# Four sums of a small tail, done one by one among the next expert's first steps

## The chip, the core and the metric

The kernel runs on one core of a Trainium2 chip. The metric is the device time of one execution in microseconds (us), less being better. The engines are PE (matrix products; PEld is its weight load), DVE (vector), ACT (activation), POOL and SP (which here mostly start DMAs). Each works through its own instructions in order; they wait for one another through semaphores. PSUM is the memory into which PE writes its results.

## What is computed

Attention with a local window and block summaries gives 3072 rows of 512; then comes a mixture of eight experts, each token going to two of them. The change lies in the experts:

```python
def _moe_ref(x, w_gate, w_noise, noise, w1, w2):
    ...
    for e in range(E):
        for k in range(2):
            mask = top2[:, k] == e
            ...
            h = np.maximum(x[mask] @ w1[e], 0.0)
            out[mask] += top2_w[mask, k, None] * (h @ w2[e])
    return out.astype(np.float32)
```

## The kernel before

Attention and the choice of experts come first (the first quarter of the time), then the experts one after the other, `e` from 0 to 7, sorted by how many tokens they have. `CAPS` (line 38) gives each a number of slots: 800, 832, 808, 800, 784, 776, 768, 768. The slots are worked in chunks of 128; what goes beyond six chunks is the **tail**, chunk 6 (`LAST`). Experts 3, 4 and 5 have tails of 32, 16 and 8 slots. Expert 0 has one of 32 as well, experts 1 and 2 have tails of 64 and 40 that go another way, and experts 6 and 7 have none.

All matrices are split into a high and a low half of 16 bits, and three products of halves make one product. The first layer of experts 2 to 7 (`seven`, line 1370) is a scheme of seven products on half-sized blocks, in four steps `i` = 0 to 3. In this document **(i,u)** is product u of step i. PE does them in this order: (0,1) and (0,5) ahead of the tail of the expert before (`seven_head`, line 1581), then, behind that tail, (0,2), (0,6), and for each i from 1 on (i,1), (i,5), (i−1,7), (i,2), (i,6), (i−1,3), (i−1,4). Each is six matmuls into a bank of PSUM. Between products, other engines read and rewrite those banks:

- after (i,2), (i,3) and (i,4), ACT writes the high half `hth` (L1392) and DVE the low half `htl` (L1395);
- after (i,6), DVE adds ACT's copy `p` of (i,5) to what stands in (i,6)'s bank and writes the sum into the bank of (i,3) (`h<-h,p`, L1386); (i,7), which goes on in (i,6)'s bank, may not start before that is done;
- after (i,7), DVE makes the sum `rh` (L1388), which ACT and DVE then halve;
- (i+2,5) starts afresh in the bank of (i,3), so it waits for both halves of (i,3).

The second layer (`mm2_part`, line 1417) makes a chunk's 128 rows in one PSUM tile `pt`. `mm2_out` (line 911) has DVE multiply it by the token's weight and add the earlier output `prev` (gathered by POOL), and POOL scatters the result `y` to the output.

For a tail of at most 32 slots (`four`, line 780) the matmuls for hidden columns f, f+4 go to a quarter of PE of their own. So the result stands as four partial sums in the four groups of 32 partitions of `pt`, and DVE adds them up: instruction `g` reads partitions 32g to 32g+n, multiplies by the weight, and adds `prev` (g = 0) or the `y` so far (L920). After the fourth comes the scatter.

The order is written out by hand. `on(t, f, ...)` puts a piece of work at place t of an expert's plan, and `hook(t)` does what stands there (pieces of one place in the order in which they were asked for). Place 3 lies behind (0,2), 4 to 6 behind (0,6), 7 and 8 behind (1,1) and (1,5), 9 behind (0,7), 10 behind (1,2), 11 behind (1,6), 12 behind (0,3), 13 behind (0,4); 14 to 20 lie likewise in the next step. DVE's other work at these places is the low halves of the expert's second-layer weights (`w2l`, L758, places 4, 7, 14, 21) and sums and low halves of the next expert's tokens (`xt`, L1293 to L1297, places 9, 11, 12; `x`, L1323, places 15, 16, 18, 19). The gathers of `prev` for the expert's first chunks stand at places 17, 20 and 23; a gather waits for the scatters of the expert before.

Of the kernel before, what the change touches and what calls it, by code (L numbers as in the profile page):

```python
# [25 lines left out]
E, F = 8, 1024  # L26
# [37 lines left out]
def attn_moe(ctx, tc, qt, kt, vt, wgn, noise, w1, w2, out):  # L64
# [23 lines left out]
    def indirect(**kw):  # L88
        nc.gpsimd.memset(spacer, 0.0)
        return nc.gpsimd.indirect_dma_start(**kw)  # L90
# [689 lines left out]
    def four(e, c):  # L780
        return c == LAST and CAPS[e] - LAST * P <= 32

    def tb_of(e, c):
        return TB0[:, c] if e == 0 and c < 3 else TB[:, e, c]
# [3 lines left out]
    def chunks(e):  # L788
        return -(-CAPS[e] // P)
# [78 lines left out]
        return lows  # L868

    ow = {}  # L870
    pi_ = [0]

    def prev_gather(e, c):
# [37 lines left out]
    def mm2_out(e, c, py, pv):  # L911
        last = c == LAST
        if four(e, c):
            n = CAPS[e] - LAST * P
            y = late[0].tile([P, DM], F32, name="y", bufs=4)[:n]
            gw = tb_of(e, c).bitcast(F32)[:n, 1:2]
            for g in range(4):
                x = py[32 * g:32 * g + n]
                if g or pv is not None:
                    nc.vector.scalar_tensor_tensor(y, x, gw, y if g else pv[:n], op0=OP.mult, op1=OP.add)  # L920
                else:
                    nc.vector.tensor_scalar(y, x, gw, None, op0=OP.mult)
            y_scatter(e, c, y)
            return
        d = HD if last else DM
        y = late[0].tile([P, DM], F32, name="y", bufs=4)[:, :d]
        gw = (TL[:, e] if last else tb_of(e, c)).bitcast(F32)[:, 1:2]
        if pv is None:
            nc.vector.tensor_scalar(y, py[:, :d], gw, None, op0=OP.mult)
        else:  # L930
            nc.vector.scalar_tensor_tensor(y, py[:, :d], gw, pv[:, :d], op0=OP.mult, op1=OP.add)  # L931
        y_scatter(e, c, y)
# [7 lines left out]
    def y_scatter(e, c, y):  # L940
        last = c == LAST and not four(e, c)
        n = CAPS[e] - LAST * P if four(e, c) else P
        s = indirect(
            out=out2 if last else out,
            out_offset=bass.IndirectOffsetOnAxis(ap=IL[:, e:e + 1] if last else tb_of(e, c)[:n, 0:1], axis=0),
            in_=y, in_offset=None, bounds_check=(2 * N if last else N) - 1, oob_is_err=False)
        for o in ow.get(e, []):
            tc.declare_no_dep(s.ins, o.ins, reason="an expert's slots hold different tokens")
        ow.setdefault(e, []).append(s)
# [449 lines left out]
    def seven_head(e):  # L1399
        if e == 2:  # L1400
            banks_init()
        seven(e, 0, 1)
        seven(e, 0, 5)
# [60 lines left out]
    def on(t, f, *a):  # L1464
        plan.setdefault(t, []).append((f, a))

    def hook(t):
        for f, a in plan.pop(t, []):
            f(*a)

    def plan_w1(n, p, t, *u):
        on(t, w_load, n, p)
        on(u[0], w1_sums, n, p)
        for i in range(2):
            on(u[1 + i], w1_hi, n, p, i)
        for i in range(2):
            on(u[3 + i], w1_lo, n, p, i)

    def plan_x(n, g, t, s, h, l):
        if t is not None:  # L1480
            on(t, xs_gather, n, g)
        for i in range(3):
            on(s[i], xs_sums, n, g, i)
        for i in range(2):
            on(h[i], xs_hi, n, g, i)
        for i in range(4):
            on(l[i], xs_lo, n, g, i // 2, i % 2)

    for e in range(1, E):
        pv = []  # L1490

        def prev():
            if len(pv) < chunks(e):
                pv.append(prev_gather(e, len(pv)))

        n = e + 1
        if e == 1:
            on(0, tail_ids)
            plan_x(n, 0, 0, (3, 3, 3), (4, 4), (5, 5, 5, 5))
            plan_x(n, 1, 1, (6, 6, 6), (7, 7), (8, 8, 8, 8))  # L1500
            plan_w1(n, 0, 1, 9, 9, 10, 10, 10)
            plan_w1(n, 1, 2, 11, 11, 12, 12, 12)
            plan_x(n, 2, 7, (13, 13, 13), (14, 14), (15, 15, 15, 15))
            plan_w1(n, 2, 11, 33, 33, 34, 34, 34)
            plan_x(n, 3, 12, (35, 35, 35), (36, 36), (37, 37, 37, 37))
            plan_w1(n, 3, 13, 38, 38, 39, 39, 39)
        else:
            for i, (a, b) in enumerate(((3, 4), (4, 7), (8, 14), (15, 21))):
                on(a, w_hi, e, 4 + i)
                on(b, w_lo, e, 4 + i)  # L1510
            on(36, tail_next, e)
            if n < E:
                plan_x(n, 0, None, (9, 11, 12), (10, 13), (15, 16, 18, 19))
                plan_x(n, 1, None, (22, 23, 25), (24, 27), (28, 29, 29, 31))
                plan_w1(n, 0, 8, 32, 32, 33, 33, 34)
                plan_w1(n, 1, 15, 35, 35, 36, 36, 37)
                plan_x(n, 2, 20, (38, 38, 38), (39, 39), (40, 40, 40, 40))
                plan_w1(n, 2, 35, 41, 41, 42, 42, 43)
                plan_x(n, 3, 32, (44, 44, 44), (45, 45), (46, 46, 46, 46))
                plan_w1(n, 3, 38, 47, 47, 48, 48, 49)  # L1520
            if e > 2:
                on(4, w_load, e, 6)
                on(4, w_load, e, 7)
        if n + 1 < E:
            on(40 if e == 1 else 43, xs_gather, n + 1, 0)
            on(42 if e == 1 else 47, xs_gather, n + 1, 1)
        if n < E:
            on(44, w_load, n, 4)
            on(44, w_load, n, 5)
        if e == 1:  # L1530
            on(48, w_load, n, 6)
            on(48, w_load, n, 7)
        for t in (17, 20, 23):
            on(t, prev)
        if e == 1:
            for half in range(2):
                for f in range(FC):
                    mm1(e, half, f)
                    hook(8 * half + f)
            for t in range(16, 32):  # L1540
                hook(t)
        else:
            hi, lo = seven(e, 0, 2)
            hi()
            lo()
            hook(3)
            seven(e, 0, 6)
            for t in range(4, 7):
                hook(t)
            for i in range(1, 5):  # L1550
                if i < 4:
                    seven(e, i, 1)
                    hook(7 * i)
                    seven(e, i, 5)
                    hook(7 * i + 1)
                h7 = seven(e, i - 1, 7)
                h7[0]()
                hook(7 * i + 2 if i < 4 else 28)
                if i < 4:
                    h2 = seven(e, i, 2)  # L1560
                    h2[0]()
                    h7[1]()
                    hook(7 * i + 3)
                    seven(e, i, 6)
                    h2[1]()
                    hook(7 * i + 4)
                else:
                    py = psum.tile([P, 512], F32, name="pt", bufs=2)
                    mm2_part(e, 0, py, 0, range(7), True, False)
                    h7[1]()  # L1570
                    hook(29)
                h3 = seven(e, i - 1, 3)
                h3[0]()
                hook(7 * i + 5 if i < 4 else 30)
                h4 = seven(e, i - 1, 4)
                h4[0]()
                h3[1]()
                h4[1]()
                hook(7 * i + 6 if i < 4 else 31)
        for c in range(chunks(e)):  # L1580
            if c == chunks(e) - 1 and n < E:
                seven_head(n)
            if c or e == 1:
                py = psum.tile([P, 512], F32, name="pt", bufs=2)
                for i, k in enumerate((0, 2, 1)):
                    if e == 1:
                        mm2_pass(e, c, py, k, 1)
                    else:
                        mm2_part(e, c, py, k, range(FC), i == 0, i == 2)
                    if i < 2:  # L1590
                        hook(32 + 3 * c + i)
            else:
                for k in (2, 1):
                    mm2_part(e, 0, py, k, range(7), False, False)
                    hook(33 - k // 2)
                for k in (0, 2, 1):
                    mm2_part(e, 0, py, k, (7,), False, k == 1)
            mm2_out(e, c, py, pv[c])
            prev()
            hook(34 + 3 * c)  # L1600
        for t in range(60):
            hook(t)
# [104 lines left out]
```

## Time and profile before

| what | value |
|---|---|
| time, median of 3 runs | 643.7 us (642.26 to 645.98) |
| profiled execution | 650.73 us |
| its span, first to last instruction | 648.9 us |
| mean granted PE clock in the span | 0.989 |

The profile is that of one execution. Its parts: the page with each engine's busy time and the chain that ended last; the timeline, in which a row has the start (us from the span's start), the length, the engine, line and operation, result and operands with their shape, the count, and in brackets the idle time of the engine just before and what ended it; and the busy time in stretches. Neighbouring instructions of one kind are one row of the timeline. PE's ends are modelled, so its waits are better read from starts.

### The profile page before, as it was taken

The numbers are of one execution on the slowest core, as the hardware profiler recorded it, in microseconds if no ns is written. First come the engines' busy times: TensorE is split into PE (matmuls) and PEld (weight loads), VectorE is DVE, ScalarE is ACT, GpSimd is POOL, SyncE is SP. The second block draws the span as 40 slices with busy tenths as digits, with TensorE's granted clock in tenths as the row PEclk, the third lists the DMA queues.
The fourth block names the chain that finished last, engine by engine and source line by source line (L and its number), as shares of the span: only waits on it lengthen the run. The fifth ranks groups of instructions, "written<-read, shape, count | busy, mean of one in ns | idle before, by whom it ended". The sixth has DMA issues, their size and how long they took to land.

```text
span 648.9 us, 14149 instructions
## 1 busy us (share of the span) xinstructions
PE 628.6 (97%) x5295; PEld 363.4 (56%) x5295; DVE 481.2 (74%) x1039; ACT 316.1 (49%) x692; POOL 250.2 (39%) x432
## 2 busy tenths in 40 slices
PE   8989898999999999999999999999999999999995
PEld 7778676765554554465446544554454455445542
DVE  5768598979887599368887887988798679767510
ACT  4878597973054354065436433653465256425300
POOL 4352043202335353623572356326632542333041
PEclk9999798999999999999999999999999999999998
DMA  9999978963639595838786688769776868763021
GB/s 304 325 278 342 307 218 275 299 230 124 198 123 252 166 220 144 282 84 170 185 226 172 168 200 246 181 135 225 236 201 136 221 210 165 175 191 123 3 94 51
DMA packets 123709, 127.93 MB, mean 197 GB/s; under 512 B 83242, under 2 KB 86674, under 8 KB 123630
## 3 DMA queue, kind: packets, MB, share of 16 engines
q1 hardware_dynamic: 111838, 90.66, 52.1%
q0 software_dynamic: 11792, 36.27, 18.2%
q8 instruction: 44, 0.72, 0.5%
q14 instruction: 35, 0.29, 0.2%
HBM read 81.85 MB, written 25.61 MB: 166 GB/s over the span
## 4 chain that ended last, share of the span: by engine, by line
PE 86%; DVE 6%; ACT 3%; DMA 2%; issue 2%; SPq 1%; POOL 0%; POOLq 0%; DVEq 0%; ACTq 0%
PE pt L1432 29%; PE h L1360 16%; PE h L854 10%; PE pt L909 7%; PE pt L1360 3%; PE pt L341 3%; PE o L1360 3%; PE s L318 3%; PE o L354 3%; PE h L909 2%; PE o L246 1%; ACT p L333 1%; PE pt L378 1%; DMA vd<-in_vt_dram 1%; DVE y L920 1%
## 5 line engine op out<-in xcount | busy, mean ns | idle before, releaser
L90 POOL DMA_INDIRECT out_dram<-y,tb x52 | 69.5, 1336 | 165.3 <-DVE y L931 127.7
L90 POOL DMA_INDIRECT xg<-xd,tb x54 | 60.9, 1127 | 118.8 <-DVE rh L1388 31.5
L1432 PEld LDWEIGHTS <-hth 128*128 128x128 f16 x576 | 56.3, 98 | 66.7
L931 DVE SCALAR_TENSOR_TENSOR y<-pt,tb,prev 128x512 f32<-128x512 f32 x42 | 31.5, 749 | 64.9 <-PE pt L1432 54.2
L1360 PEld LDWEIGHTS <-w1h 128*128 128x128 f16 x504 | 48.9, 98 | 38.2 <-issue 4.4
L1432 PE MATMUL pt<-w2l,hth 128*128 128x512 f16 x288 | 69.0, 379 | 0.0
L1432 PE MATMUL pt<-w2h,htl 128*128 128x512 f16 x288 | 69.0, 379 | 0.0
L1432 PE MATMUL pt<-w2h,hth 128*128 128x512 f16 x288 | 69.0, 379 | 0.0
L1360 PEld LDWEIGHTS <-w1l 128*128 128x128 f16 x504 | 49.3, 98 | 34.9
L90 POOL DMA_INDIRECT prev<-out_dram,tb x45 | 52.6, 1169 | 23.9 <-issue 13.2
L333 ACT ACTIVATE p<-s,nm 128x120 f32<-128x120 f32 x192 | 51.1, 377 | 0.8
L854 PE MATMUL h<-xte,w1h 128*128 128x384 f16 (+2 forms) x248 | 49.1, 336 | 0.0
L1432 PEld LDWEIGHTS <-htl 128*128 128x128 f16 x288 | 28.2, 98 | 34.0
L1349 ACT ACTIVATE w1h<-stg 128x768 f16<-128x768 f32 (+1 forms) x24 | 22.7, 944 | 40.6 <-DVE stg L1340 40.6
L1392 ACT ACTIVATE hth<-h 128x384 f16<-128x384 f32 (+4 forms) x48 | 23.8, 497 | 35.5 <-PE h L1360 35.5
L1349 ACT ACTIVATE w1l<-stg 128x768 f16<-128x768 f32 (+1 forms) x24 | 22.5, 942 | 37.3 <-DVE stg L1340 37.3
L1360 PE MATMUL h<-xte,w1h 128*128 128x384 f16 (+4 forms) x180 | 39.7, 329 | 0.7 <-DVE h L1386 0.4
L1360 PE MATMUL h<-xte,w1l 128*128 128x384 f16 (+4 forms) x180 | 39.7, 329 | 0.0
L1313 ACT ACTIVATE x<-xt 128x512 f16<-128x512 f32 (+2 forms) x44 | 26.5, 626 | 23.4 <-issue 19.2
L1340 DVE TENSOR_TENSOR stg<-stg 128x256 f32<-128x256 f32 x96 | 36.3, 419 | 0.8
L344 ACT ACTIVATE pts<-pt 120x512 f32<-120x512 f32 x48 | 26.7, 609 | 19.4 <-PE pt L341 19.4
L854 PEld LDWEIGHTS <-w1h 128*128 128x128 f16 x256 | 24.7, 98 | 19.5 <-issue 1.2
(301 smaller groups left out, 1305.7 us busy)
## 6 DMA issues: line engine op xcount, KB each, us to landing
stg<-in_w_dram SPq DMA_DIRECT2D x64, 512.0 KB
q<-in_qt_dram SPq DMA_DIRECT2D x24, 256.0 KB
xd<-x SPq DMA_DIRECT2D x24, 256.0 KB
out_dram<-xg SPq DMA_DIRECT2D x8, 768.0 KB
kb<-in_kt_dram SPq DMA_DIRECT2D x6, 768.0 KB
hth<-in_vt_dram SPq DMA_DIRECT2D x12, 260.0 KB
htl<-in_vt_dram SPq DMA_DIRECT2D x16, 195.0 KB
ve<-in_vt_dram SPq DMA_DIRECT2D x12, 260.0 KB
```

Of the source, the lines that this page charges most:

```text
L90: return nc.gpsimd.indirect_dma_start(**kw)
L333: nc.scalar.activation(PE_[t][:, a, hp, :], SC[t][:, a, hp, :], AF.Exp, bias=NM[t][:, 1, a, hp:hp + 1], scale=0.125)
L344: nc.scalar.activation(PT[t][:NK, a], pt[:NK], AF.Copy)
L854: nc.tensor.matmul(ph[:, :n], w1_of(w, wn, c, f), x[:, xo + c, c0:c1], start=(k == 0), stop=(k == 11))
L909: nc.tensor.matmul(py, hx[:, f, c * P:c * P + P], wv[:, f, :], start=st, stop=sp)
L931: nc.vector.scalar_tensor_tensor(y, py[:, :d], gw, pv[:, :d], op0=OP.mult, op1=OP.add)
L1313: nc.scalar.activation(t[:r, c:c + k], src, AF.Copy)
L1340: nc.vector.tensor_tensor(o, x, y, op=op)
L1349: nc.scalar.activation(hi, x, AF.Copy, scale=W1S)
L1360: nc.tensor.matmul(ph[:, :h], w[:, la, a, P * j:P * j + P], x[:, j, :h], start=start and k == 0, stop=k == 5, skip_group_check=True)
L1392: nc.scalar.activation(hh[:, f, t], src, AF.Relu)
L1432: nc.tensor.matmul(py, x, wv[:, f, :], start=st, stop=sp, skip_group_check=True)
```

## The change

For tails of at most 32 slots of the experts 1 to 6 (in effect 3, 4 and 5) `mm2_out` no longer asks for the four sums and the scatter. It keeps four closures in `late_sums`, and the plan of the next expert takes them up at places 5, 8, 10 and 13; the scatter comes with the fourth. The tail of expert 0 stays as it was.

```diff
     ow = {}
+    late_sums = []
     pi_ = [0]
...
             n = CAPS[e] - LAST * P
             y = late[0].tile([P, DM], F32, name="y", bufs=4)[:n]
             gw = tb_of(e, c).bitcast(F32)[:n, 1:2]
-            for g in range(4):
+
+            def part(g):
                 x = py[32 * g:32 * g + n]
                 if g or pv is not None:
                     nc.vector.scalar_tensor_tensor(y, x, gw, y if g else pv[:n], op0=OP.mult, op1=OP.add)
                 else:
                     nc.vector.tensor_scalar(y, x, gw, None, op0=OP.mult)
-            y_scatter(e, c, y)
+                if g == 3:
+                    y_scatter(e, c, y)
+
+            for g in range(4):
+                if 0 < e < E - 1:
+                    late_sums.append((part, g))
+                else:
+                    part(g)
             return
...
                 on(a, w_hi, e, 4 + i)
                 on(b, w_lo, e, 4 + i)
+            for t in (5, 8, 10, 13):
+                if late_sums:
+                    f, g = late_sums.pop(0)
+                    on(t, f, g)
             on(36, tail_next, e)
```

The order of instructions shows it on DVE. Line numbers of the changed kernel are 9 higher from here on (L1395 becomes L1404; L920 becomes L922). At the end of expert 4, DVE had this before; `y` is the sum, `pt_6513` the tail's result, `htl<-o` belongs to (0,2) of expert 5, `h<-h,p_6511` to (0,6), `rh` and `htl<-rh` to (0,7), `h<-h,p_6584` to (1,6):

```order
L920 SCALAR_TENSOR_TENSOR y_6538<-pt_6513,tb_182,prev0_2968 16x512
L920 SCALAR_TENSOR_TENSOR y_6538<-pt_6513,tb_182,y_6538 16x512 x3
L1395 SCALAR_TENSOR_TENSOR htl_90<-o_2882,hth_89 128x388
L1386 TENSOR_TENSOR h_4482<-h_4480,p5_6511 128x388
L758 SCALAR_TENSOR_TENSOR w2l0_322<-stg_6408,w2h0_321 128x1024
L758 SCALAR_TENSOR_TENSOR w2l0_322<-stg_6410,w2h0_321 128x1024
L1388 TENSOR_TENSOR rh1_3827<-h_4480,p5_6511 128x388
L1293 TENSOR_TENSOR xt_6607<-xg0_165 128x512
L1395 SCALAR_TENSOR_TENSOR htl_90<-rh1_3827,hth_89 128x388
L1386 TENSOR_TENSOR h_4483<-h_4481,p5_6584 128x388
```

All four sums stood ahead of everything of the new expert. At the same place it now has:

```order
L1404 SCALAR_TENSOR_TENSOR htl_90<-o_2882,hth_89 128x388
L1395 TENSOR_TENSOR h_4482<-h_4480,p5_6511 128x388
L758 SCALAR_TENSOR_TENSOR w2l0_322<-stg_6408,w2h0_321 128x1024
L922 SCALAR_TENSOR_TENSOR y_6538<-pt_6513,tb_182,prev0_2968 16x512
L758 SCALAR_TENSOR_TENSOR w2l0_322<-stg_6410,w2h0_321 128x1024
L922 SCALAR_TENSOR_TENSOR y_6538<-pt_6513,tb_182,y_6538 16x512
L1397 TENSOR_TENSOR rh1_3827<-h_4480,p5_6511 128x388
L1302 TENSOR_TENSOR xt_6601<-xg0_165 128x512
L1404 SCALAR_TENSOR_TENSOR htl_90<-rh1_3827,hth_89 128x388
L922 SCALAR_TENSOR_TENSOR y_6538<-pt_6513,tb_182,y_6538 16x512
L1395 TENSOR_TENSOR h_4483<-h_4481,p5_6577 128x388
```

Sums 0, 1 and 2 have moved behind the add of (0,6), into the stretch that ends with the low half of (0,3). The second place is a little further on, again on DVE; before, behind that low half (the first row, of (0,3); the second is of (0,4)):

```order
L1395 SCALAR_TENSOR_TENSOR htl_90<-h_4482,hth_89 128x388
L1395 SCALAR_TENSOR_TENSOR htl_90<-h_4480,hth_89 128x388
L758 SCALAR_TENSOR_TENSOR w2l0_322<-stg_6565,w2h0_321 128x1024
L1323 TENSOR_TENSOR x_6669<-xg0_165,x_6618 128x512
L1388 TENSOR_TENSOR rh1_3827<-h_4481,p5_6584 128x388
```

and now:

```order
L1404 SCALAR_TENSOR_TENSOR htl_90<-h_4482,hth_89 128x388
L1404 SCALAR_TENSOR_TENSOR htl_90<-h_4480,hth_89 128x388
L922 SCALAR_TENSOR_TENSOR y_6538<-pt_6513,tb_182,y_6538 16x512
L758 SCALAR_TENSOR_TENSOR w2l0_322<-stg_6557,w2h0_321 128x1024
L1332 TENSOR_TENSOR x_6669<-xg0_165,x_6613 128x512
L1397 TENSOR_TENSOR rh1_3827<-h_4481,p5_6577 128x388
```

Sum 3 stands behind the two low halves, and the scatter waits for it. On POOL, ACT and SP the order of instructions is unchanged, and on PE too.

## The prediction

> **What bounds the kernel now.** The page's first part: how long each engine is busy.
>
> ```profile
> PE 628.6 (97%) x5295; PEld 363.4 (56%) x5295; DVE 481.2 (74%) x1039; ACT 316.1 (49%) x692; POOL 250.2 (39%) x432
> ```
>
> PE is the bound, so an edit on DVE is worth what it adds to or takes from PE's idle time, and no more. The change touches three places, the starts of experts 4, 5 and 6. The busy time in stretches shows them. A row has the stretch, its length, then the busy time of PE, PEld, DVE, ACT and POOL with their instructions, the granted clock, and DMA. Rows 1 to 3 run from product (0,2) of the new expert to product (2,5), ten products later; row 4 is the same stretch of expert 3, which follows a tail without the four sums; rows 5 to 7 run over the seven products from (2,5) to (3,5).
>
> ```profile
> 403.89:414.47 10.58, 10.28 (x64) 5.87 (x61) 10.16 (x17) 7.42 (x14) 2.10 (x4) 1.00 0.62 192
> 464.94:475.49 10.55, 10.19 (x65) 5.88 (x61) 10.13 (x17) 7.42 (x14) 2.65 (x4) 1.00 0.61 195
> 525.78:536.29 10.51, 10.08 (x64) 5.88 (x61) 10.10 (x17) 7.42 (x14) 2.20 (x4) 1.00 0.51 170
> 342.91:353.07 10.16, 10.16 (x62) 5.89 (x61) 8.13 (x14) 7.30 (x13) 2.47 (x4) 1.00 0.58 178
> 414.47:421.43 6.96, 6.96 (x42) 4.10 (x42) 6.40 (x12) 4.30 (x8) 3.38 (x6) 1.00 0.83 179
> 475.49:482.38 6.89, 6.89 (x42) 4.10 (x42) 6.36 (x12) 4.24 (x8) 3.35 (x6) 1.00 0.84 190
> 536.29:543.13 6.84, 6.84 (x42) 4.10 (x42) 6.34 (x12) 4.21 (x8) 3.30 (x6) 1.00 0.87 162
> ```
>
> Rows 5 to 7 have no PE idle, so a product takes 0.994, 0.984 and 0.977 us there. Ten would take 9.94, 9.84 and 9.77 and take 10.58, 10.55 and 10.51: PE loses 0.64 + 0.71 + 0.74 = **2.1 us** in all. That is the most the change can give. DVE is busy 10.1 of these 10.5 us; expert 3 has 8.1 and no loss.
>
> For expert 5, whose (0,2) starts at 464.94, the timeline of PE shows the two waits, and that of DVE the queue behind it (start, length, instruction, idle time before it and its releaser).
>
> ```profile
> 469.27 0.82 PE L1360 MATMUL h<-w2l,w1h 128*128 128x388 f16 x4 [0.21 <-DVE h L1386]
> ...
> 475.49 0.82 PE L1360 MATMUL h<-w2l,w1h 128*128 128x388 f16 x4 [0.15 <-DVE htl L1395]
> ```
>
> ```profile
> 465.06 0.74 DVE L920 SCALAR_TENSOR_TENSOR y<-pt,tb,prev 16x512 f32<-16x512 f32 x1 [1.51 <-PE pt L1426]
> 465.84 2.31 DVE L920 SCALAR_TENSOR_TENSOR y<-pt,tb,y 16x512 f32<-16x512 f32 x3
> 468.18 0.56 DVE L1395 SCALAR_TENSOR_TENSOR htl<-o,hth 128x388 f16<-128x388 f32 x1
> 468.65 0.56 DVE L1386 TENSOR_TENSOR h<-h,p 128x388 f32<-128x388 f32 x1
> 469.12 2.35 DVE L758 SCALAR_TENSOR_TENSOR w2l<-stg,w2h 128x1024 f16<-128x1024 f32 x2
> 471.39 0.55 DVE L1388 TENSOR_TENSOR rh<-h,p 128x388 f32<-128x388 f32 x1
> ...
> 472.67 0.56 DVE L1395 SCALAR_TENSOR_TENSOR htl<-rh,hth 128x388 f16<-128x388 f32 x1
> 473.15 0.56 DVE L1386 TENSOR_TENSOR h<-h,p 128x388 f32<-128x388 f32 x1
> ...
> 474.88 1.02 DVE L1395 SCALAR_TENSOR_TENSOR htl<-h,hth 128x388 f16<-128x388 f32 x2
> ```
>
> The sums push `htl<-o` and the add behind it; the add ends late and product (0,7) with it. From 468.18 DVE never catches up, and (2,5), which overwrites the bank that `htl<-h` (the low half of (0,3)) reads, starts 0.61 us after that instruction does (474.88, 475.49). This is the place that decides.
>
> **The first wait goes.** Expert 3 shows when `htl<-o` can start with a free DVE: 344.68 − 342.91 = 1.77 us after (0,2).
>
> ```profile
> 344.68 0.57 DVE L1395 SCALAR_TENSOR_TENSOR htl<-o,hth 128x400 f16<-128x400 f32 x1 [1.17 <-ACT hth L1392]
> ```
>
> In expert 5 it starts 3.24 after (468.18 − 464.94), so it gains 1.47 us, and (0,7), due 3.94 after, no longer waits for the add, which ends 2.25 + 0.56 after.
>
> **Three sums come in ahead of the second wait.** By the rows of DVE's order, sums 0, 1 and 2 now stand between the add and `htl<-h`. What one costs in a queue:
>
> ```profile
> 461.67 0.75 DVE L931 SCALAR_TENSOR_TENSOR y<-pt,tb,prev 128x512 f32<-128x512 f32 x1
> 462.34 1.21 DVE L1353 SCALAR_TENSOR_TENSOR w1l<-stg,w1l 128x1024 f16<-128x1024 f32 x1
> ```
>
> ```profile
> 58.44 1.21 DVE L265 COPY hth<-pt 24x130 f32<-24x130 f32 x4 [0.33 <-issue]
> ...
> 65.44 0.29 DVE L406 COPY lt<-o 128x128 f32<-128x128 f32 x1 [0.42 <-PE o L354]
> 65.65 0.15 DVE L363 TENSOR_SCALAR r<-o 128x8 f32<-128x8 f32 x1
> ```
>
> ```profile
> 466.14 0.49 ACT L1392 ACTIVATE hth<-o 128x388 f16<-128x388 f32 x1 [2.00 <-PE o L1360]
> ```
>
> A full chunk's instruction of the same size lets the next start after 0.67 of its 0.75 us. The tail's last sum does not: the three end at 465.84 + 2.31 = 468.15, and `htl<-o` starts at 468.18, although it takes nothing from them and ACT's instruction that it waits for was done at 466.63. The four copies of the attention stage behave alike: they read PSUM at partitions 0, 32, 64 and 96 and start 0.30 apart at 0.29 each, where a copy of 0.29 between readers of the same partitions takes 0.21. So an instruction that reads PSUM in another group of 32 partitions than the last reader seems to wait for the end. Sum g reads group g, all else in this stretch group 0. Ends: 0.67 a sum and nothing around it, or 0.79 (0.745 + 0.045) for every sum and the full length of the instruction ahead of it. I take the full wait where the group changes: sum 0 at 0.67, sums 1 and 2 at 0.79, and the instructions ahead of those two at 1.26 for 1.13 (`w2l`) and 0.61 for 0.48 (`htl`). No row shows whether an instruction without PSUM in between (these two, and `x` ahead of `rh` further down) breaks the wait; if it does, each of the three is 0.13 less.
>
> VectorE: DVE Perf Modes of the Trainium skill, in its section "Two Vector instructions with no wait between them", has this as a model: an instruction is held until all before it have finished when its input begins in another group of 32 partitions than the last one read from that memory, whatever ran in between. By it the sum is 4.6, as below; if what runs in between broke it, 4.6 − 9 × 0.13 = 3.4. It speaks against this change: four switches of group at each place become six.
>
> DVE of expert 5, counted from (0,2): `htl<-o` 1.77, add 2.25, `w2l` 2.72, sum 0 3.85, `w2l` 4.52, sum 1 5.78, `rh` 6.57, `htl<-rh` 7.85 (1.28 after `rh`, as in 471.39 to 472.67: ACT is between), sum 2 8.46, add 9.25, `htl<-h` 10.98 (1.73 later, as before), (2,5) **11.59**. Against 10.58, 10.55 and 10.51: +1.01, +1.04, +1.08 = **+3.1 us**. PE needs no more than 9.94, so the wait is real.
>
> **The fourth sum.** Behind (2,5):
>
> ```profile
> 475.82 1.22 DVE L758 SCALAR_TENSOR_TENSOR w2l<-stg,w2h 128x1024 f16<-128x1024 f32 x1
> 476.95 0.68 DVE L1323 TENSOR_TENSOR x<-xg,x 128x512 f16<-128x512 f32 x1
> 477.65 0.56 DVE L1388 TENSOR_TENSOR rh<-h,p 128x388 f32<-128x388 f32 x1
> ...
> 478.81 0.56 DVE L1395 SCALAR_TENSOR_TENSOR htl<-rh,hth 128x388 f16<-128x388 f32 x1 [0.26 <-ACT hth L1392]
> 479.62 0.57 DVE L1386 TENSOR_TENSOR h<-h,p 128x388 f32<-128x388 f32 x1 [0.25 <-PE h L1360]
> ...
> 481.77 1.02 DVE L1395 SCALAR_TENSOR_TENSOR htl<-h,hth 128x388 f16<-128x388 f32 x2
> ```
>
> The last `htl<-h` starts 0.61 ahead of (3,5) at 482.38: again no slack at all, only PE happened not to be late. DVE has about 0.5 us idle on the way. Counted from (2,5): second `htl<-h` −0.13, sum 3 at 0.47 (its group changes), `w2l` 1.14, `x` 2.27, `rh` 3.00 (again a change), `htl<-rh` 4.16, add 4.64, `htl<-h` 6.79 (2.15 later, as 479.62 to 481.77), (3,5) **7.40**. Against 6.96, 6.89 and 6.84: +0.44, +0.51, +0.56 = **+1.5 us**. With no wait for a group it is 7.14, +0.7. From (3,5) on DVE stands to PE as before.
>
> **The scatter.** Sum 3 ends at 464.94 + 11.59 + 0.47 + 0.75 = 477.75, 9.6 us later than before (468.15), and the scatter with it.
>
> ```profile
> 470.80 1.60 POOL L90 DMA_INDIRECT prev<-out_dram,tb  x1 [1.42 <-DMA out_dram<-y,tb]
> ```
>
> ```profile
> 496.90 0.74 DVE L931 SCALAR_TENSOR_TENSOR y<-pt,tb,prev 128x512 f32<-128x512 f32 x1
> ```
>
> POOL's order stays, and SP gets nothing new. Behind the scatter stands the gather of the next expert's first `prev`, which waits for its landing (the releaser in its row): from 470.80 to about 480.4, done at 482; it is needed at 496.90. The gathers behind it move by some 4 us and are needed later still. I cost this at nothing; its cover is 10 us.
>
> **Sum.** 3.1 + 1.5 = +4.6 us. The profiled execution takes 650.73 (span 648.9) and would take 655.3; it is 7.0 above the median of the runs, 643.7, whose time becomes **648.3**. Without any wait for a group: 1.6 + 0.7 = +2.4, 646.1. With one around every sum (0.24 more before (2,5), 0.12 behind): +5.7, 649.4.
>
> **Rivals.** *Hidden sums, faster:* the sums fit into DVE's gaps, both waits go, −2.1: 641.6. Perfetto Trace Analysis of the Trainium skill, "Optimizing Scalar/DVE Operations", has it that an engine that is not saturated but makes others wait can help by smaller pieces. It decides whether DVE has 2 us idle between the add and `htl<-h`. For it: 1.47 are freed, and DVE is at 74% over the span. Against it: what is freed lies ahead of `htl<-o`, where no sum now stands, and behind it the queue has at most 0.2 us of gaps. *Cheap sums, about the same:* +2.4, 646.1; for it, no row has a sum away from another one. *The scatter's delay reaches `prev`:* from 10 us late on each further us is lost; one us at each place gives 648.3 + 3 = 651.3; no row comes near. That the sums stay where they were is excluded by DVE's order.
>
> **Chances.** A difference under 0.5% (3.2 us) can hardly be told from none here. Forecast (+3.4 to +5.7) 0.62, cheap sums 0.18, hidden 0.10, scatter or something else late 0.10. Slower by over 0.5%: most of the first, a little of the second, the last: 0.68. Faster: a third of the hidden case, 0.03. Same: 0.29. The range is 646.1 to 649.4, widened by half the spread of the three runs (1.9): 644.2 to 651.3.
>
> **What would show it.** Right: no PE wait ahead of (0,7); (2,5) some 11.6 after (0,2) and released by `htl`, (3,5) 7.4 after (2,5); sums 1 and 2 taking 0.79 until the next start; `prev` in time. Wrong: ten products in 9.8 (hidden), or `rh` starting 0.67 after sum 1 (cheap).

## The result, and the profile after

The changed kernel takes **648.83 us** (median of 10 runs, 647.0 to 654.38), the kernel before 644.42 (10 runs, 642.03 to 647.07). The ratio is 1.0062, with a 95% interval of 1.0035 to 1.0089: slower by 4.4 us (2.3 to 5.7 by the interval), where +4.6 us and 648.3 us were forecast. A second measurement (e8, below) gave 1.0055 (1.0024 to 1.0086).

The page's first part, after, in answer to the line of before:

```profile
PE 624.0 (97%) x5295; PEld 360.1 (56%) x5295; DVE 481.6 (75%) x1039; ACT 316.3 (49%) x692; POOL 254.9 (39%) x432
```

The page doesn't tell the kernels apart: the same instructions, and shares that differ by one per cent at most. The profiled span is even shorter (645.8 against 648.9 us); the granted clock was 0.997 on the mean in this execution and 0.989 in the one of before, which was granted 0.83 from 60 to 80 us, in the attention stage. So no spans are compared here, only stretches in which the clock was 1.00 in both. The busy time in stretches, after, has the same columns as that of the kernel before. Rows 1 to 3 run from (0,2) to (2,5) of the experts 4, 5 and 6, rows 4 to 6 from (2,5) to (3,5):

```profile
396.68:408.18 11.50, 10.12 (x64) 5.88 (x61) 9.49 (x16) 7.74 (x14) 0.00 (x0) 1.00 0.50 159
459.06:470.53 11.47, 10.03 (x64) 5.89 (x61) 9.48 (x16) 7.72 (x14) 0.00 (x0) 1.00 0.51 162
521.28:532.71 11.43, 9.93 (x65) 5.88 (x62) 9.46 (x16) 7.70 (x14) 0.00 (x0) 1.00 0.46 141
408.18:415.56 7.38, 7.13 (x43) 4.10 (x43) 7.05 (x13) 3.97 (x8) 2.89 (x3) 1.00 0.57 136
470.53:477.88 7.35, 7.06 (x42) 4.10 (x42) 7.03 (x13) 3.95 (x8) 3.82 (x4) 1.00 0.57 135
532.71:540.02 7.31, 6.98 (x42) 4.10 (x42) 6.99 (x13) 3.93 (x8) 2.28 (x2) 1.00 0.71 137
sum 56.44, PE 51.24 PEld 29.96 DVE 49.50 ACT 35.01 POOL 8.99; mean PE 8.54 PEld 4.99 DVE 8.25 ACT 5.83 POOL 1.50
```

Before, the six stretches took 31.64 + 20.69 = 52.33 us; now 56.44: **+4.11 us**, of the 4.4 by which the medians differ. The first three grew by 0.92 each (11.50 − 10.58, and so on), the others by 0.42, 0.46 and 0.47. The 0.3 us that are left lie within the interval. From (3,5) to the second layer both kernels take the same, 6.96, 6.89 and 6.83 us, so there is no third place.

The waits of PE for DVE at these places, totalled over the span (what waited, for whom: us, times, longest). Before:

```profile
PE h L1360 <- DVE h L1386: 0.6, 3, 0.2
PE h L1360 <- DVE htl L1395: 0.3, 2, 0.2
```

And after:

```profile
PE h L1369 <- DVE htl L1404: 5.2, 6, 1.5
```

The wait for the add, ahead of (0,7), is gone. The six waits are two at each of the three places. The two of expert 5 in PE's timeline are (2,5) and (3,5):

```profile
470.53 0.82 PE L1369 MATMUL h<-w2l,w1h 128*128 128x388 f16 x4 [1.44 <-DVE htl L1404]
...
477.88 0.82 PE L1369 MATMUL h<-w2l,w1l 128*128 128x388 f16 x4 [0.29 <-DVE htl L1404]
```

And DVE's timeline ahead of them, from the low half of (0,2), which starts at 459.06:

```profile
460.79 0.56 DVE L1404 SCALAR_TENSOR_TENSOR htl<-o,hth 128x388 f16<-128x388 f32 x1 [3.11 <-ACT hth L1401]
461.27 0.56 DVE L1395 TENSOR_TENSOR h<-h,p 128x388 f32<-128x388 f32 x1
461.74 1.22 DVE L758 SCALAR_TENSOR_TENSOR w2l<-stg,w2h 128x1024 f16<-128x1024 f32 x1
462.87 0.73 DVE L922 SCALAR_TENSOR_TENSOR y<-pt,tb,prev 16x512 f32<-16x512 f32 x1
463.54 1.20 DVE L758 SCALAR_TENSOR_TENSOR w2l<-stg,w2h 128x1024 f16<-128x1024 f32 x1
464.77 0.74 DVE L922 SCALAR_TENSOR_TENSOR y<-pt,tb,y 16x512 f32<-16x512 f32 x1
465.54 0.56 DVE L1397 TENSOR_TENSOR rh<-h,p 128x388 f32<-128x388 f32 x1
466.02 0.68 DVE L1302 TENSOR_TENSOR xt<-xg 128x512 f32<-128x512 f32 x1
466.83 0.56 DVE L1404 SCALAR_TENSOR_TENSOR htl<-rh,hth 128x388 f16<-128x388 f32 x1
467.41 0.75 DVE L922 SCALAR_TENSOR_TENSOR y<-pt,tb,y 16x512 f32<-16x512 f32 x1
468.18 0.57 DVE L1395 TENSOR_TENSOR h<-h,p 128x388 f32<-128x388 f32 x1
...
469.92 1.02 DVE L1404 SCALAR_TENSOR_TENSOR htl<-h,hth 128x388 f16<-128x388 f32 x2
470.98 0.75 DVE L922 SCALAR_TENSOR_TENSOR y<-pt,tb,y 16x512 f32<-16x512 f32 x1
471.66 1.20 DVE L758 SCALAR_TENSOR_TENSOR w2l<-stg,w2h 128x1024 f16<-128x1024 f32 x1
472.79 0.67 DVE L1332 TENSOR_TENSOR x<-xg,x 128x512 f16<-128x512 f32 x1
473.50 0.56 DVE L1397 TENSOR_TENSOR rh<-h,p 128x388 f32<-128x388 f32 x1
...
477.27 1.02 DVE L1404 SCALAR_TENSOR_TENSOR htl<-h,hth 128x388 f16<-128x388 f32 x2
```

Read it by two things. The first row has **3.11 us of idle time** ahead of it: before, the sums began 0.12 us after (0,2) and `htl<-o` came 3.24 after it, so now 1.6 of the 3.1 us in which they ran lie idle (459.18 to 460.79). From there to 469.92, the start of the instruction that (2,5) waits for, no row has idle time marked, DVE is busy for 8.86 of the 9.13 us, and three sums stand in that stretch. Half of the time of the sums had been free; now three of them stand in a queue that has next to no gap.

### The profile page after: what moved, and what is told of

The parts are those of the page before. It is cut to its first block, busy times and chain, and to the rows that moved or that the text cites. A ratio compares the mean times of both kernels' runs of the same rounds, so it can differ in the third digit from the quotient of the medians.

```text
span 645.8 us, 14149 instructions
## 1 busy us (share of the span) xinstructions
PE 624.0 (97%) x5295; PEld 360.1 (56%) x5295; DVE 481.6 (75%) x1039; ACT 316.3 (49%) x692; POOL 254.9 (39%) x432
## 4 chain that ended last, share of the span: by engine, by line
PE 79%; DVE 10%; issue 3%; DMA 3%; ACT 3%; SPq 1%; POOL 0%; POOLq 0%; DVEq 0%; ACTq 0%
PE pt L1441 29%; PE h L1369 14%; PE h L854 8%; PE pt L910 7%; PE o L1369 3%; PE pt L1369 3%; PE pt L341 2%; PE s L318 2%; PE h L910 2%; PE o L354 2%; DVE htl L1404 2%; DVE nm L325 1%; PE pt L378 1%; DVE y L922 1%; DMA kb<-in_kt_dram 1%
## 5 line engine op out<-in xcount | busy, mean ns | idle before, releaser
L90 POOL DMA_INDIRECT out_dram<-y,tb x52 | 72.8, 1399 | 184.6 <-DVE y L940 118.1
L1404 DVE SCALAR_TENSOR_TENSOR htl<-h,hth 128x384 f16<-128x384 f32 (+4 forms) x48 | 26.4, 563 | 11.8 <-ACT hth L1401 11.5
```

The source lines that it names most:

```text
L1404: nc.vector.scalar_tensor_tensor(hl[:, f, t], src, 0.0, hh[:, f, t], op0=OP.max, op1=OP.subtract)
```

## The experiments

The table has, for each traced kernel and the experts 4 / 5 / 6, the starts of (0,7) and (2,5) after (0,2) and of (3,5) after (2,5), all from PE's timeline, and the sum of the last two over the three experts (the length of the six stretches). The times stand with each experiment.

| kernel | (0,7) | (2,5) | (3,5) | sum |
|---|---|---|---|---|
| before | 4.34 / 4.33 / 4.32 | 10.58 / 10.55 / 10.51 | 6.96 / 6.89 / 6.84 | 52.33 |
| changed | 3.99 / 3.95 / 3.91 | 11.50 / 11.47 / 11.43 | 7.38 / 7.35 / 7.31 | 56.44 |
| e1 one group | 3.99 / 3.95 / 3.91 | 11.03 / 10.99 / 10.96 | 7.11 / 7.09 / 7.06 | 54.24 |
| e2 scatter alone late | 4.33 / 4.32 / 4.88 | 10.57 / 10.54 / 11.08 | 6.97 / 6.90 / 6.84 | 52.90 |
| e3 sum 3 at 13 | 3.99 / 3.95 / 4.16 | 9.96 / 9.86 / 10.35 | 7.25 / 7.24 / 7.33 | 51.99 |
| e4 sum 3 at 20 | 3.99 / 3.95 / 4.08 | 9.96 / 9.87 / 10.28 | 6.96 / 6.89 / 6.85 | 50.81 |
| e5 before, again | 4.34 / 4.32 / 4.32 | 10.58 / 10.54 / 10.51 | 6.97 / 6.90 / 6.84 | 52.34 |
| e6 all four at 5 | 3.99 / 3.96 / 3.91 | 12.19 / 12.16 / 12.15 | 6.96 / 6.89 / 6.85 | 57.20 |
| e7 as e4 | 3.99 / 3.95 / 3.91 | 9.96 / 9.86 / 9.76 | 6.97 / 6.89 / 6.85 | 50.29 |
| e8 changed, again | 3.99 / 3.95 / 3.91 | 11.50 / 11.47 / 11.42 | 7.37 / 7.34 / 7.32 | 56.42 |
| e9 as e4 | 3.99 / 3.95 / 4.25 | 9.96 / 10.00 / 10.46 | 6.97 / 6.89 / 6.84 | 51.12 |
| e10 before, again | 4.40 / 4.45 / 5.07 | 10.64 / 10.68 / 11.26 | 6.97 / 6.89 / 6.84 | 53.28 |

The theory: DVE's queue ahead of the two low halves decides, and in it the sums cost their 0.67 us and the switch between groups of 32 partitions. Its rivals: the switch costs nothing there, or the late scatter is what is paid for.

**e1, the switch of group.** Against the changed kernel, all four sums read the same partitions:

```diff
-                x = py[32 * g:32 * g + n]
+                x = py[0:n]
```

The kernel leaves out the other three partial sums; everything else stays.

> The changed kernel with one thing left out of the computation: all four sums read the tail's first group of 32 partitions, so the other three partial sums are not added. Same instructions, same places, same lengths. Theory (an instruction that reads PSUM in another group of partitions than the last reader waits for the end of all before it): the instruction ahead of sum 1 (w2l) gives way after about 1.13 instead of 1.23 us, sum 1 and sum 2 after 0.67 instead of 0.77, the instruction ahead of sum 2 after 0.48 instead of 0.58; (2,5) starts some 11.1 us after (0,2) of expert 5 instead of 11.47, (3,5) some 7.1 to 7.2 after (2,5) instead of 7.35. Over three places about 1.7 us less than the changed kernel, +2.3 us against the kernel before. Rival (sums are this dear wherever they read): nothing moves, +4 us.

Measured: 648.41 us (12 runs) against 646.94 of the kernel before (35), ratio 1.0024 (0.9993 to 1.0054). That interval reaches from no difference to almost the whole loss, so the starts have to decide. The stretches take 54.24 in place of 56.44: **2.2 us** go. DVE's timeline of e1, expert 5, at the same instructions (neighbouring rows):

```profile
464.23 1.20 DVE L758 SCALAR_TENSOR_TENSOR w2l<-stg,w2h 128x1024 f16<-128x1024 f32 x1
465.36 0.73 DVE L922 SCALAR_TENSOR_TENSOR y<-pt,tb,y 16x512 f32<-16x512 f32 x1
466.02 0.54 DVE L1397 TENSOR_TENSOR rh<-h,p 128x388 f32<-128x388 f32 x1
...
467.29 0.56 DVE L1404 SCALAR_TENSOR_TENSOR htl<-rh,hth 128x388 f16<-128x388 f32 x1
467.77 0.73 DVE L922 SCALAR_TENSOR_TENSOR y<-pt,tb,y 16x512 f32<-16x512 f32 x1
468.43 0.55 DVE L1395 TENSOR_TENSOR h<-h,p 128x388 f32<-128x388 f32 x1
```

From start to start: `w2l` to sum 1 1.13 us here, 1.23 in the changed kernel; sum 1 to `rh` 0.66 and 0.77; `htl` to sum 2 0.48 and 0.58; sum 2 to the add 0.66 and 0.77. Each instruction at a switch starts about 0.1 us later. So the switch is real, and it is about half of the loss. The other half, 54.24 − 52.33 = +1.9, is what the sums cost in a full queue without it.

**e2, the scatter alone.** The sums stand in front as before; only the scatter waits for place 13:

```diff
-                if g == 3:
-                    y_scatter(e, c, y)

             for g in range(4):
-                if 0 < e < E - 1:
-                    late_sums.append((part, g))
-                else:
-                    part(g)
+                part(g)
+            if 0 < e < E - 1:
+                late_sums.append((lambda g: y_scatter(e, c, y), 3))
+            else:
+                y_scatter(e, c, y)
...
-            for t in (5, 8, 10, 13):
+            for t in (13,):
```

> The four sums where they were before, only the scatter is asked for at place 13 of the next expert. Theory (the whole cost is DVE's queue): POOL's order is that of before, so nothing moves: 0 us, the waits of (0,7) and (2,5) as before (10.55 from (0,2) to (2,5)). Rival (the late scatter costs through the gathers behind it or through DMA traffic): up to +4 us without any change on DVE.

Measured: 647.26 us (10 runs) against 646.94, ratio 1.0003 (0.9972 to 1.0033). The starts of experts 4 and 5 are those of the kernel before to 0.01 us. At expert 6, (0,7) and (2,5) come 0.56 and 0.57 later. That isn't the late scatter's doing: below, e7 has a late scatter too, on another chip, and doesn't show it, and e10 shows it in the kernel before, without a late scatter. The late scatter costs nothing that these runs resolve.

**e3, three sums back in front.** Only sum 3 and the scatter wait for place 13:

```diff
-                if 0 < e < E - 1:
+                if 0 < e < E - 1 and g == 3:
...
-            for t in (5, 8, 10, 13):
+            for t in (13,):
```

> Sums 0 to 2 stay in front as before, only sum 3 and the scatter go to place 13. Theory (what counts is DVE's work between the start of the expert and the low half of (0,3), and then up to (3,5)): the first low half starts some 2.45 us after (0,2) instead of 3.24, neither (0,7) nor (2,5) waits (9.84 from (0,2) to (2,5) in expert 5), but (3,5) starts 7.35 instead of 6.89 after (2,5). Three places: -2.1 + 1.4 = -0.7 us, not to be told from none by the time but plain in the starts. Rival (spreading as such is what costs, each sum away from the others its 1 us or more): slower than before by over 1 us.

Measured: 645.31 us (10 runs) against 646.94, ratio 0.9983 (0.9953 to 1.0013). In experts 4 and 5 (2,5) comes 9.96 and 9.86 after (0,2), which is PE's own pace: the three sums were the whole loss there, and even the wait of the kernel before is gone. (3,5) still comes 0.29 and 0.35 late against the kernel before: sum 3 at place 13 costs by itself, as DVE has less idle time between (2,5) and (3,5) than the sum takes. At expert 6, where the delay of e2 and e10 comes on top, (2,5) takes 10.35 and (3,5) is 0.49 late.

**e4, e7 and e9, sum 3 behind both narrow places.** As e3, but sum 3 and the scatter stand at place 20, and the gathers of `prev`, which must come after that scatter, go from places 17, 20, 23 to 20, 21, 23 where a sum is late (against the changed kernel):

```diff
-                if 0 < e < E - 1:
+                if 0 < e < E - 1 and g == 3:
...
         n = e + 1
+        tp = (17, 20, 23)
...
-            for t in (5, 8, 10, 13):
+            for t in (20,):
                 if late_sums:
+                    tp = (20, 21, 23)
                     f, g = late_sums.pop(0)
...
-        for t in (17, 20, 23):
+        for t in tp:
             on(t, prev)
```

> As the last, but sum 3 and the scatter go to place 20, behind the second narrow point (3,5), and the gathers of the earlier output follow it at 20, 21, 23. Theory: (2,5) 9.84 after (0,2) and (3,5) 6.89 after (2,5) in expert 5, no wait in any of the three places: -2.1 us against the kernel before, 0.3%. Rivals: the sum makes a third narrow point behind (3,5), in front of (3,7) or the second layer, +0.4 us a place there; or the gathers of the earlier output, now some 7 us later than before, come late for the first chunk, and the first chunk's sum waits.

> The kernel with sums 0 to 2 in front and sum 3 with the scatter at place 20 again, for its time: by the starts read so far 1.5 to 2.1 us less than the kernel before, 0.2 to 0.3%.

> The same kernel as in the two runs with sum 3 and the scatter at place 20 (sums 0 to 2 in front), which gave ratios of 0.9989 and 0.9966 with intervals that overlap. If PE's idle time at the three places is all that counts, it is faster than the kernel before by the 2.0 us that the traces show there (sum of the starts 50.29 against 52.33): ratio 0.997. If the later scatter and the moved gathers give part of it back further on: 0.999 to 1.000. In the trace: (0,7) 3.9 after (0,2), (2,5) 9.96, 9.86 and 9.76 after (0,2), (3,5) 6.97, 6.89 and 6.85 after (2,5), and no wait of PE for low halves.

Measured, each time beside runs of the kernel before on the same chip: 645.84 against 646.94, ratio 0.9989 (0.9962 to 1.0017); 642.04 against 644.36, 0.9966 (0.9936 to 0.9996); 646.10 against 647.53, 0.9984 (0.9957 to 1.0012). All three lean to faster, by 1.1 to 2.3 us; only the second interval leaves 1 out, and the third holds both 0.997 and 0.999 to 1.000, so it doesn't decide whether the later gathers give something back. The starts of e9 were not all as expected: (2,5) of expert 5 comes 10.00 after (0,2) in place of 9.86, and at expert 6, in e4 as in e9, PE still waits 0.19 us for a low half ahead of (2,5), with the delay that e10 shows below. The busy time in stretches of e7, same stretches as above:

```profile
397.81:407.77 9.96, 9.96 (x64) 5.88 (x61) 9.57 (x16) 7.24 (x13) 0.00 (x0) 1.00 0.51 167
458.25:468.11 9.86, 9.86 (x65) 5.87 (x61) 9.48 (x16) 7.22 (x13) 0.00 (x0) 1.00 0.54 173
518.40:528.16 9.76, 9.76 (x64) 5.87 (x61) 9.38 (x16) 7.17 (x13) 0.00 (x0) 1.00 0.47 155
407.77:414.74 6.97, 6.97 (x45) 4.10 (x43) 6.29 (x12) 4.48 (x9) 0.00 (x0) 1.00 0.67 151
468.11:475.00 6.89, 6.89 (x43) 4.10 (x42) 6.25 (x12) 4.46 (x9) 0.00 (x0) 1.00 0.70 156
528.16:535.01 6.85, 6.85 (x45) 4.10 (x43) 6.31 (x12) 4.46 (x9) 0.00 (x0) 1.00 0.79 161
sum 50.29, PE 50.29 PEld 29.93 DVE 47.29 ACT 35.03 POOL 0.00; mean PE 8.38 PEld 4.99 DVE 7.88 ACT 5.84 POOL 0.00
```

PE's busy time is the length of every row: the 2.04 us (52.33 − 50.29) that the kernel before lost here, by PE's starts, are gone, and that is all there was. DVE isn't less busy for it: 9.57 us in the first row, 9.49 in that of the changed kernel, and the next two differ by at most 0.08. The scatter is later still, and the first `prev` is nevertheless there for its first use at 489.51. The timelines of POOL and DVE in e7:

```profile
476.49 2.21 POOL L90 DMA_INDIRECT out_dram<-y,tb  x1 [18.66 <-DVE y L922]
...
481.68 1.00 POOL L90 DMA_INDIRECT prev<-out_dram,tb  x1 [0.22 <-issue]
```

```profile
489.51 0.75 DVE L940 SCALAR_TENSOR_TENSOR y<-pt,tb,prev 128x512 f32<-128x512 f32 x1
```

**e5 and e8, both kernels again,** without an edit, on the chip of e6 and e7:

> The kernel before, unchanged, profiled on the chip of the runs beside it, as a control: at the place of expert 6 the profiles of the runs with sums in front show sum 0 starting 0.67 to 0.75 us after (0,2), the kernel before 0.12. If that belongs to the chip or the execution, it may show here too; if it belongs to the late scatter, which those runs had in common, it stays at 0.12. In experts 4 and 5: (2,5) at 10.58 and 10.55 after (0,2).

> The changed kernel again, on the same chip as the last: by the starts 4.1 us more than the kernel before, 0.6%; (2,5) at 11.47 after (0,2) and (3,5) at 7.35 after (2,5) in expert 5.

Measured: 644.53 us (one run) and 648.57 us (12 runs) against 644.36 (23 runs). Every start in the table repeats to 0.02 us, so on this chip the differences between the kernels' starts belong to the kernels. In e5 the first sum of expert 6 starts 0.12 us after (0,2), as in the first trace of this kernel. By itself that would also fit a delay by the late scatter; but e7, with a late scatter on the same chip, has 0.12 too.

**e6, all four sums at place 5.** It asks whether spreading the sums is what costs, or that they stand behind the add at all:

```diff
-            for t in (5, 8, 10, 13):
+            for t in (5, 5, 5, 5):
```

> All four sums and the scatter at place 5, one behind the other, nothing at 8, 10 and 13. Theory (DVE's queue by starts, 0.775 from sum to sum, 0.67 after the last one since the next instruction does not read PSUM, the second w2l giving way after 1.23 since rh then reads another group): in expert 5 sum 0 at 3.81, rh at 8.0, low half of (0,3) at 11.5, (2,5) at 12.1 after (0,2); a new wait of PE ahead of (0,4), some 0.8 us, since rh is late; (3,5) back at 6.89 after (2,5). So 0.2 us a place more than the changed kernel. Rival (spreading the sums is what costs, a stretch of sums in a row is cheap): (2,5) at 10.6 or less, as in the kernel before.

Measured: 649.58 us in one run. (2,5) comes 12.15 to 12.19 after (0,2), (3,5) loses nothing. PE's timeline of e6, expert 5, where (0,2) starts at 460.71; the rows are (0,4) and (2,5):

```profile
469.38 0.82 PE L1369 MATMUL h<-w2l,w1h 128*128 128x388 f16 x4 [0.61 <-DVE rh L1397]
...
472.87 0.82 PE L1369 MATMUL h<-w2l,w1h 128*128 128x388 f16 x4 [1.36 <-DVE htl L1404]
```

One block has four switches of group where the spread sums have six, but it puts the fourth sum, too, ahead of (2,5), and makes a new wait for `rh`. The sum is 57.20, 0.8 more than spread out. So it is not the spreading that is dear: the cost lies in standing behind the add, and a block there is dearer still.

**e10, the kernel before on a chip where expert 6 starts late,** without an edit:

> The kernel before once more, for the late results at the tail of expert 5: in the runs where the copy of (0,5) came 2.9 to 3.1 us after the product's start in place of 1.2, (0,7) and (2,5) of expert 6 came 0.2 to 0.7 us later too. If that belongs to a chip or an execution and not to an order of sums, it can stand in this trace too: (0,7) near 4.9 and (2,5) near 11.1 after (0,2). If it belongs to the edits, this trace reads 4.32 and 10.51, as the two others of this kernel do, and the copy comes after 1.2 us at all three places.

Measured: 650.99 us (one run, against 645.69 to 652.38 in five others on that chip). (0,7) of expert 6 comes 5.07 and (2,5) 11.26 after (0,2): what e2 showed there stands in the kernel before as well, with its own order of sums. Experts 4 and 5 come 0.06 to 0.14 later than in the other traces of this kernel; why, no run shows. e9 ran on that chip, too, and its sum is 53.28 − 51.12 = 2.16 less; on the chip of e5 and e7 the difference is 52.34 − 50.29 = 2.05. On the chip of e1 to e4 no trace of the kernel before was taken; e2, which has its order on DVE, stands 52.90 − 50.81 = 2.09 above e4.

## Why the prediction was right, point by point

- **The bound and the place.** Right. PE's waits at the three places carry the loss: 4.11 of the 4.4 us lie there. That the time came within 0.5 us of 648.3 is in part luck, as the kernel before measured 0.7 us more over ten runs (644.42) than over the three that the forecast started from (643.7), and the stretches grew by 0.5 less than said. Sums taken out of the queue ahead of (2,5) end the loss there (e3), and the last one taken out of that ahead of (3,5) ends the other (e4).
- **The first wait goes.** Right: `htl<-o` starts 1.73 us after (0,2) (460.79 − 459.06; 1.77 was said), (0,7) at 3.95 (3.94), with no wait.
- **Three sums ahead of (2,5).** Right, a little too large: +0.92 at each place, 2.76 in all, for +3.1. Of the 0.12 us by which expert 5's (2,5) comes earlier than said (11.47 for 11.59), 0.04 is the earlier `htl<-o`; the rest is the price of a switch, which I had from the length plus a margin. Sum 1 to `rh` takes 0.77 where 0.79 was taken, the held `w2l` 1.23 (1.26), the held `htl` 0.58 (0.61).
- **The open point, whether an instruction without PSUM breaks the wait.** It doesn't: `w2l`, which reads no PSUM, stands between sum 0 and sum 1, and sum 1 waits for its end (463.54 + 1.20 + 0.03). The section "Two Vector instructions with no wait between them" of VectorE: DVE Perf Modes in the Trainium skill has, as a model, the wait hang on the group in which the input of the last instruction to read that memory began, whatever ran in between; this case's trace agrees (`w2l` to sum 1 1.23 us here, 1.13 in e1, where the group stays). The case in which `w2l`, `htl` and `x` break it, +3.4, and that of "cheap sums", +2.4, fall with it. The case of cheap sums is what e1 measures, +1.9 by the starts.
- **The fourth sum.** Right: 0.42 to 0.47 at each place, 1.35 us in all for +1.5. In e3, where (2,5) isn't held up, it alone costs 0.29 and 0.35 at experts 4 and 5.
- **The scatter costs nothing.** Right: POOL's timeline of the changed kernel has it at 472.01, 12.95 us after (0,2), and the gather of `prev` behind it starts 17.2 us after (0,2), 1.7 later than said, which is still 16 us ahead of its use, at 492.39 in DVE's timeline, where DVE doesn't wait; e2 delays the scatter alone, e7 delays it further, and neither shows a cost.

```profile
472.01 2.22 POOL L90 DMA_INDIRECT out_dram<-y,tb  x1 [13.37 <-DVE y L922]
...
476.25 1.44 POOL L90 DMA_INDIRECT prev<-out_dram,tb  x1 [1.93 <-DMA out_dram<-y,tb]
```

```profile
492.39 0.74 DVE L940 SCALAR_TENSOR_TENSOR y<-pt,tb,prev 128x512 f32<-128x512 f32 x1
```

- **Hidden sums.** Fell: DVE has no idle time between the add and `htl<-h`. That smaller pieces may help where an engine that isn't saturated holds up others, as Perfetto Trace Analysis of the Trainium skill has it in "Optimizing Scalar/DVE Operations", did not come about here: DVE is at 75% over the span, but the pieces came into a stretch in which it was busy for 8.86 of 9.13 us. The 2.1 us that were named as the most that can be had are to be had by another order: sums 0 to 2 in front, the last behind (3,5), where e7 shows PE without idle time. With sum 3 gone from the front, `htl<-o` starts 2.44 after (0,2) in e7, early enough for (0,7).

What stays open: the traces show 2.05 to 2.16 us less for that order, the three measurements 1.1 to 2.3. They agree within their intervals, but only one of them by itself shows it to be faster.

## What to carry to other kernels

Before work is moved off an engine's queue, look at the idle time ahead of it: half of what these sums took was free where they stood, and next to nothing was where three of them went. Count the queue back from each instruction that the bounding engine waits for; where it has no gap, each instruction put ahead of that place costs its full time, however low the engine's share over the span is. What may be late (here the last sum and its scatter, with 10 us and more in hand) goes behind the last such place, not to the next free-looking one.

## What the runs showed of the hardware

**The switch of group has a price that was measured apart:** e1 and the changed kernel differ in nothing else, and 2.20 us over three places is 0.73 us a place. There are six switches at a place, so 0.12 us each. Row by row in expert 5, the changed kernel less e1: sum 1 0.10, `rh` 0.11, sum 2 0.10, the add 0.11, sum 3 0.12, the second `rh` 0.11. In all these rows the held instruction starts behind the end of the one ahead of it, as sum 1 does 0.03 us after `w2l` in the changed kernel; in e1 sum 1 starts 0.07 us ahead of that end. The price doesn't need a neighbour that reads PSUM: `x` stands ahead of the second `rh` and reads none.

**On two of the experiments' three chips the results of PE at the tail of expert 5 came late, though its recorded starts did not.** In e10, ACT's copy of (0,5) and the first sum, by the timelines of PE, ACT and DVE:

```profile
523.17 0.81 PE L1360 MATMUL h<-xte,w1h 128*128 128x384 f16 x4
```

```profile
526.29 0.49 ACT L1384 ACTIVATE p<-h 128x384 f32<-128x384 f32 x1 [1.01 <-PE pt L1426]
```

```profile
526.52 0.74 DVE L920 SCALAR_TENSOR_TENSOR y<-pt,tb,prev 8x512 f32<-8x512 f32 x1 [2.24 <-PE pt L1426]
```

The copy starts 3.12 us after the product (526.29 − 523.17), where it was 1.17 in the first trace of the kernel before. On the chip of e1 to e4 it was 2.92 to 3.02, on that of e9 and e10 3.10 and 3.12, on that of e5 to e8 1.18, at the same recorded distances of PE's starts (tail to (0,2) 1.41 us in all). It goes with the chip, not with an edit, in all ten traces of the experiments, and costs kernels with sums in front 0.5 to 0.8 us at (2,5) of expert 6 (e2, e3, e4, e9 and e10 in the table). What holds the results back no run here shows.
